# Two-layer recurrent attention with dense layers: the tokens' values loaded behind the transfer that turns P

## The chip, the cores and the metric

The kernel runs on one core of a Trainium2 chip. The metric is the time of one execution in device microseconds (us), as the median of several runs. A profile of one execution stands beside it: all rows of instructions, waits and DMA transfers below are from that one.

## The reference, cut to what matters

There are four layers: attention with a recurrent memory (A), a dense layer with a ReLU (B), A again and B again, each on the layer norm of its input and added to it. A works on segments of 32 tokens, one after another. The memory of 8 rows that a segment hands on is the first 8 rows of its output.

```python
for s in range(n_seg):                              # 64 segments of 32 tokens
    h = concat([mem, xs], axis=1)                   # 8 + 32 = 40 rows of 512
    q, k, v = (einsum('btd,dhe->bhte', h, W) for W in (Wq, Wk, Wv))   # 32 heads of 128
    p = softmax(where(mask, einsum(q, k) * scale, -1e9))
    o = einsum('bhte,hed->btd', einsum('bhqk,bhke->bhqe', p, v), Wo)
    mem, out_s = o[:, :8], o[:, 8:]
```

The segments of one layer form a chain through `mem`; B has no such chain.

## The kernel before, in words

The kernel goes through 68 steps. In step k the first attention layer (a = 0) works on segment k, and the second (a = 1) on segment k - 4, so that steps 4 to 63 hold both layers ("two-layer steps", 60 of them), and steps 0 to 3 and 64 to 67 hold one (`single`). Rows 0 to 39 of a tile belong to layer 0, rows 64 to 103 to layer 1. The order of the work on PE (TensorE), DVE (VectorE), SP (the queue that issues nearly all DMAs) and POOL (GpSimd) is the order in which the program is written; each engine takes its instructions in that order and waits at each for what it needs. ACT's (ScalarE's) order is left to the planner, by priority.

A two-layer step runs like this (lines in brackets):

- queries and keys of heads 0 to 15, from `HT` (`qk`, L575), into PSUM and out through ACT (L581) and DVE (L583);
- SP: the values of the tokens come into `Vs` from DRAM (`load_values`, L734). Values of tokens don't depend on the chain and are worked out steps ahead: for layer 0 in `values0` (L296, stored at L313 into `vd0`), or by riding along with the memory values (`vmds`), for layer 1 in `values1` at the end of the step before (L341, stored at L351 into `vd1`). `load_values` issues one DMA for layer 1 (L737), and for layer 0 one (L746) where k%4 is 2 or 3, or two (L742) where k%4 is 0 or 1. In all 512 KB come into `Vs`, in pieces of 1 KB;
- SP: the normalized rows are turned into `xnT` by a DMA transpose (`transpose_step`, L289), for the dense layer (`dense_h`, L507) and for tokens of later steps; then the values of the memory rows, just stored by `memory_values` (L770), come into the other rows of `Vs` (`load_memory_values`, L775, four DMAs of 32 KB);
- scores of heads 0 to 15 (L609) and their exponentials;
- queries and keys of heads 16 to 31. Behind their first batch, `probabilities` stands: it finishes the softmax of the first half (POOL writes `P_sb`, L646) and has SP turn it by a DMA transpose into `PT0` (`turn_p`, L663). Where k%4 is 3, `inputs_T` has SP turn the next inputs too (L248); `load_x` loads input rows from POOL's queue (L120);
- the dense layer, and the output matmuls of the step before (`output_x`, L365) or, where k%4 is 1, values of later tokens (`values0`, L306, and its stores, L313);
- scores and softmax of the second half, turned on PE (`transpose_p`, L656);
- `weighted_v` (L682): P times V. This reads `PT0`, `PT_sb` and `Vs`, whose rows are the weights that PE loads;
- the output matmul of the memory rows (L617), the new memory (`new_memory`, L820), the values of the next step's memory rows (L765), and the next step.

Of the kernel before, what the change touches and what calls it, by code (L numbers as in the profile page):

```python
# [22 lines left out]
def kernel(  # L23
# [48 lines left out]
    def has1(k):  # L72
        return DELTA <= k <= LAST
# [30 lines left out]
    def load_xb(n):  # L104
        tag, bufs = ("vst", 5) if n in (1, 2, 3) else ("xb", 1)
        xbs[n] = wk.tile([128, Dm], BF, tag=tag, bufs=bufs, name="xb")
        nc.sync.dma_start(out=xbs[n][:], in_=A_x[0, 128 * n:128 * n + 128, :])
# [117 lines left out]
    def normalize(eng, dst, src, mom, lo, hi):  # L225
        mv, rstd = mom
        eng.tensor_scalar(out=dst[lo:hi, :], in0=src[lo:hi, :], scalar1=mv[lo:hi, 0:1], scalar2=rstd[lo:hi, 0:1],
                          op0=ALU.subtract, op1=ALU.mult)

    def moments_x(n):  # L230
        stats = wk.tile([128, 6], F32, tag="ln_stats", bufs=1)
        nc.vector.bn_stats(out=stats[:], in_=xbs[n][:])
        return stat_tail(stats, "x")
# [47 lines left out]
    def layers(k):  # L281
        return [a for a in range(2) if (has0, has1)[a](k)]
# [306 lines left out]
    def qk(hf, act, between=None, behind=None):  # L589
        res = []  # L590
        for n, (o, nh) in enumerate(BATCHES):
            res.append((o, nh) + tuple(qk_batch(n, 16 * hf + o, nh, act[0], act[-1] + 1, None if n else between)))
            if n == 0 and behind:
                behind()
            if hf and n > 0:
                masks(*act[n - 1:n])
        return res
# [64 lines left out]
    def turn_p():  # L662
        nc.sync.dma_start_transpose(out=PT0[:], in_=P_sb[:].rearrange("p s k -> p (s k)"))  # L663
# [70 lines left out]
    def load_values(k, act):  # L734
        for a in act:
            if a == 1 or k == 1:
                nc.sync.dma_start(out=Vs[64 * a + M:64 * a + L, :].rearrange("t (n e) -> t n e", n=NCH),  # L737
                            in_=(vd1.pop(k) if a else vd0[0])[:].rearrange("i j t e -> t (i j) e"))
            elif k >= 4 and k % 4 < 2:
                for u in range(2):  # L740
                    lo = M + 2 * M * u
                    nc.sync.dma_start(out=Vs[lo:lo + 2 * M, :].rearrange("t (n e) -> t n e", n=NCH),  # L742
                                in_=vmds[k - k % 4 - 4 + 2 * (k % 4) + u][:, :, 2 * M:32, :].rearrange("i j t e -> t (i j) e"))
            else:
                r = SEG * (k % 2)
                nc.sync.dma_start(out=Vs[M:L, :].rearrange("t (n e) -> t n e", n=NCH),  # L746
                            in_=vd0[k // 2][:, :, r:r + SEG, :].rearrange("i j t e -> t (i j) e"))
# [8 lines left out]
    def memory_values(k, stage=(None, None), part=range(2)):  # L756
        if 0 in part:
            vmds[k] = dram.tile([2, 4, 32, 512], BF, tag="vmd", bufs=7, name="vmd")
        vmd = vmds[k]
        for ii in part:  # L760
            vp = ps_c.tile([128, 512], F32, tag="c", name="vm")
            for c4 in range(NC4):
                for j in range(4):
                    n = 4 * ii + j
                    nc.tensor.matmul(vp[32 * j:32 * j + 32, :], lhsT=HTm[:, c4, :],  # L765
                                     rhs=Wv_sb[:, c4, n * 512:(n + 1) * 512],
                                     start=(c4 == 0), stop=(c4 == NC4 - 1), tile_position=(0, 32 * j))
            VmS = wk.tile([128, 512], BF, tag="vst", bufs=5, name="VmS")[:] if stage[ii] is None else stage[ii]
            nc.scalar.copy(out=VmS, in_=vp[:])  # L769
            nc.sync.dma_start(out=vmd[ii].rearrange("j t e -> (j t) e"), in_=VmS)  # L770
# [124 lines left out]
    def step(k):  # L895
        act = layers(k)
        single = len(act) == 1
        cont = [a for a in act if k - DELTA * a + 1 < NSEG]
        n_x = k // 4 + 3
        has_x = n_x < NXT  # L900
        by_pe = k in (1, LAST)
        ahead = has1(k + 1) or not cont
        if k % 4 == 0 and has_x:
            load_xb(n_x)
        with tc.high_priority(offset=PRIO):
            behind = norm_rows.pop(k, None)
            if k == 1:
                def behind():
                    normalize(nc.vector, xbs[n_x], xbs[n_x], moments_x(n_x), 0, 128)
            qks = qk(0, act, behind=behind)  # L910
            load_values(k, act)
            if k == 1:
                memory_values(k)
                inputs_T(n_x, True)
        part = 4 if k == LAST else 8 if single else 5
        mid = 8 if k == LAST else 16

        light = split(k)
        block(k, 0, part)
        with tc.high_priority(offset=PRIO):  # L920
            transpose_step(k)
            load_memory_values(k, act)
            scores(qks, act)
            ess = exponentials(act)

        def probabilities():

            softmax(0, act, by_pe, ess)
            if not by_pe:
                turn_p()  # L930
            if k % 4 == 3 and has_x:
                inputs_T(n_x)
            if has0(k + 1):
                load_x(k + 1)
            if k == 1:
                load_dense()

        with tc.high_priority(offset=PRIO):
            qks = qk(1, act, behind=probabilities)
        if single:  # L940
            block(k, part, mid)
        elif light:
            dense_h(k - 2, slice(0, 1))
            block(k, part, 16)
        else:
            dense_h(k - 2)
        with tc.high_priority(offset=PRIO):
            scores(qks, act)
            softmax(1, act, by_pe)
        if single:  # L950
            dense_h(k - 2, slice(0, 1) if k == LAST else slice(None))
            block(k, mid, H)
            if k == LAST:
                keep_busy(3)
        elif light:
            dense_h(k - 2, slice(1, None))
            block(k, 16, H)
        else:
            block(k, part, H)
        f_mid = 9 if ahead or k == 2 else 5  # L960
        if k < LAST:
            dense_y(k - 2, 0, f_mid)
        if not single:
            add_output(k - 1)
        if k == LAST:
            add_last(k - 1, 0)
        if k % 4 == 1 and k > 1 and has_x:
            mom["x"] = moments_x(n_x)
        with tc.high_priority(offset=PRIO):
            transpose_p(1)  # L970
        if ahead and k < LAST:
            dense_y(k - 2, f_mid, NFC)
        tokens_in(k + 1)
        if k < LAST and spare_T(k + 1) is not None:
            nc.gpsimd.tensor_copy(out=HTm[:, :, 2 * M:32], in_=spare_T(k + 1))
        with tc.high_priority(offset=PRIO):
            pvs = weighted_v(act)
            outputs(k, pvs)
        if single and k < LAST and ahead:
            add_dense(k - 2)  # L980
            store(k - 2)
        if k == LAST:
            add_last(k - 1, 1)
            last_rows(k - 1, nc.gpsimd)
        elif single:
            add_output(k - 1, 0)
        if cont:
            with tc.high_priority(offset=PRIO):
                pool, tag = (ps_c, "c") if single else (ps_wo, "wo")
                wo = pool.tile([128, Dm], F32, tag=tag, name="wo")  # L990
                output_mem(k, wo)
        if not ahead:
            dense_y(k - 2, f_mid, NFC)
        if not single and k < LAST and ahead:
            add_dense(k - 2)
            store(k - 2)
        if cont:
            with tc.high_priority(offset=PRIO):
                new_memory(k, cont, wo)
        if single and k < LAST:  # L1000
            add_output(k - 1, 1)
        if not ahead:
            add_dense(k - 2)
            store(k - 2)
        values1(k + 1, 1)
        if cont:
            output_ride(k)
            with tc.high_priority(offset=PRIO):
                memory_values(k + 1)
        with tc.high_priority(offset=PRIO):  # L1010
            prepare(k + 1)
        if k % 4 == 2 and k > 2 and has_x:
            normalize(nc.vector, xbs[n_x], xbs[n_x], mom["x"], 0, 128)
# [88 lines left out]
```

## Time and profile before

| what | value |
|---|---|
| median of 3 runs | 1600.38 us (1595.73 to 1601.42) |
| the profiled execution | 1596.61 us; its span, first to last instruction, 1594.8 us |
| granted TensorE clock | 1.000 |
| busy: PE, PEld, DVE, ACT, POOL | 98%, 83%, 80%, 46%, 22% of the span |
| DMA queue q1 (SP's transfers) | 136.09 MB, 37.6% of 16 engines' span |
| DMA queue q8 (instructions) | 335 packets of 16 KB, 5.49 MB |
| from one step's first read of `Vs` on PE to the next's | 23.0 to 23.6 us in most two-layer steps |

How to read it: PE is TensorE's matmuls, PEld its weight loads, which overlap them. SPq is SP's own sequence of instructions, where the issue of a DMA stands with the time that the issue took; when the bytes move and land is not in that row. A DMA's landing is the last update of its semaphore in the trace. The share of DMA in a row of windows is the mean busy share of 16 DMA engines. "A <- B" names what an engine waited for.

### The profile page before, as it was taken

To read this page: it belongs to the slowest core of one execution; us is meant where nothing else is said; L and a number is where in the kernel's file an instruction comes from. 1 tells how busy PE (TensorE), PEld (TensorE's weight loads), DVE (VectorE), ACT (ScalarE), POOL (GpSimd) and SP (SyncE) were. 2 spreads that over 40 slices of the span, in tenths; PEclk is the share of its full clock that TensorE was granted. 3 is DMA by queue.
4 is the path that set the end of the run, shared out by engine and by line. 5 is a ranking of instruction groups with operands and counts; after the bars stand their busy time and mean duration, and the time that the engine had idled before them with its cause. 6 is when DMAs were issued, how large, how long until landed. Compare 5 with 4: busy or idle time off the path is not lost.

```text
span 1594.8 us, 94682 instructions
## 1 busy us (share of the span) xinstructions
PE 1565.9 (98%) x42680; PEld 1320.7 (83%) x42680; DVE 1268.4 (80%) x3115; ACT 738.9 (46%) x1799; POOL 349.8 (22%) x670
## 2 busy tenths in 40 slices
PE   6999999999999999999999999999999999999998
PEld 4677888888898888889888888988888898898886
DVE  4578888888888888888888888888878888887866
ACT  3434444444544544454454545445454544545433
POOL 2012222222222222222222222222222222222110
PEclk9999999999999999999999999999999999999999
DMA  9733343343343534444334443343443333233332
GB/s 369 237 78 74 76 87 89 65 98 86 77 78 83 94 64 95 84 73 87 83 87 71 98 83 77 84 83 82 80 98 79 74 88 79 78 77 93 70 75 41
DMA packets 222564, 146.38 MB, mean 92 GB/s; under 512 B 124008, under 2 KB 216528, under 8 KB 222160
## 3 DMA queue, kind: packets, MB, share of 16 engines
q1 hardware_dynamic: 218992, 136.09, 37.6%
q8 instruction: 335, 5.49, 1.5%
q0 software_dynamic: 3072, 4.20, 1.1%
q14 instruction: 69, 0.57, 0.1%
q10 hardware_dynamic: 96, 0.03, 0.0%
HBM read 65.41 MB, written 45.35 MB: 69 GB/s over the span
## 4 chain that ended last, share of the span: by engine, by line
PE 96%; DMA 2%; DVE 1%; SPq 1%; issue 0%; ACT 0%; POOL 0%; POOLq 0%; ACTq 0%
PE qp L575 38%; PE wox L365 10%; PE wo L617 8%; PE vm L765 7%; PE v L346 7%; PE hp L507 6%; PE sp L528 5%; PE pv L682 4%; PE sp L609 4%; PE vp L306 3%; DMA Wv_sb<-in_A_Wv_dram 2%; PE tp L656 1%; PE xp L478 1%; PE wox L388 1%; SPq L134 0%; PE mt L820 0%
## 5 line engine op out<-in xcount | busy, mean ns | idle before, releaser
L581 ACT CAST QT<-qp 128x480 bf16<-128x480 f32 (+3 forms) x408 | 201.7, 494 | 392.3 <-PE qp L575 392.2
L575 PE MATMUL qp<-HT,Wq_sb 128*128 128x80 bf16 (+1 forms) x8704 | 370.2, 200 | 2.1 <-POOL HT L754 1.2
L575 PE MATMUL qp<-HT,Wk_sb 128*128 128x80 bf16 (+1 forms) x8704 | 369.2, 199 | 1.5 <-DMA Wk_sb<-in_A_Wk_dram 0.7
L575 PEld LDWEIGHTS <-Wq_sb 128*128 128x128 bf16 x8704 | 325.6, 100 | 33.8 <-issue 26.5
L575 PEld LDWEIGHTS <-Wk_sb 128*128 128x128 bf16 x8704 | 328.2, 100 | 2.3 <-DMA Wk_sb<-in_A_Wk_dram 1.2
L583 DVE CAST KT<-qp 128x480 bf16<-128x480 f32 (+3 forms) x408 | 231.4, 568 | 124.0 <-PE qp L575 118.1
L646 POOL TENSOR_TENSOR P_sb<-es,sm 128x320 bf16<-128x320 f32 x185 | 130.9, 721 | 751.7 <-ACT es L631 502.2
L365 PE MATMUL wox<-Wo_sb,OTx 128*64 128x256 bf16 x2880 | 173.6, 273 | 0.0
L625 DVE TENSOR_REDUCE mx<-sp 128x8 f32<-128x320 f32 x256 | 115.0, 487 | 73.6 <-PE sp L609 72.7
L365 PEld LDWEIGHTS <-OTx 128*64 128x64 bf16 x2880 | 150.2, 110 | 2.9
L631 ACT ACTIVATE es<-es 128x320 f32<-128x320 f32 x256 | 110.7, 469 | 58.2 <-DVE es L629 57.2
L765 PE MATMUL vm<-Wv_sb,HTm 128*32 128x512 bf16 x2176 | 136.4, 380 | 0.6 <-DVE HT L834 0.6
L641 DVE TENSOR_REDUCE sm<-es 128x8 f32<-128x320 f32 x256 | 118.3, 462 | 15.0 <-ACT es L631 4.7
L617 PE MATMUL wo<-Wo_sb,OTm 128*32 128x512 bf16 x2144 | 128.9, 380 | 0.2 <-issue 0.2
L346 PE MATMUL v<-Wv_sb,xnT 128*32 128x512 bf16 x2048 | 129.0, 378 | 0.0
L601 DVE CAST sp<-maskb 128x320 f32<-128x320 bf16 x256 | 118.4, 484 | 0.0
L629 DVE TENSOR_TENSOR es<-sp,mx 128x320 f32<-128x320 f32 x256 | 113.8, 483 | 1.5
L765 PEld LDWEIGHTS <-HTm 128*32 128x32 bf16 x2176 | 90.6, 96 | 27.4 <-issue 12.3
L528 PE MATMUL sp<-w_sb,hT 128*64 128x256 bf16 (+4 forms) x1452 | 104.1, 275 | 0.2 <-issue 0.2
L769 ACT CAST VmS<-vm 128x512 bf16<-128x512 f32 x134 | 78.6, 587 | 53.8 <-PE vm L765 53.8
L507 PE MATMUL hp<-xnT,w_sb 128*128 128x64 bf16 (+3 forms) x2948 | 102.2, 193 | 0.5 <-DVE xnT L436 0.4
L507 PEld LDWEIGHTS <-w_sb 128*128 128x128 bf16 (+1 forms) x2948 | 95.1, 101 | 1.3 <-issue 0.7
(124 smaller groups left out, 2028.8 us busy)
## 6 DMA issues: line engine op xcount, KB each, us to landing
Vs<-vd SPq DMA_DIRECT2D x96, 256.0 KB
vd<-vst SPq DMA_DIRECT2D x181, 128.0 KB
vmd<-VmS SPq DMA_DIRECT2D x134, 128.0 KB
Vs<-vmd SPq DMA_DIRECT2D x254, 32.0 KB
Vs<-vmd SPq DMA_DIRECT2D x60, 128.0 KB
Wq_sb<-in_A_Wq_dram SPq DMA_DIRECT2D x2, 2048.0 KB
Wk_sb<-in_A_Wk_dram SPq DMA_DIRECT2D x2, 2048.0 KB
Wv_sb<-in_A_Wv_dram SPq DMA_DIRECT2D x2, 2048.0 KB
```

The lines of the kernel that those rows point to most:

```text
L346: nc.tensor.matmul(vp[32 * j:32 * j + 32, :], lhsT=tokens[:, c4, :], rhs=Wv_sb[:, c4, n * 512:(n + 1) * 512], start=(c4 == 0), stop=(c4 == ...
L365: nc.tensor.matmul(out[64 * j:64 * j + nr, 0:256], lhsT=lhsT, rhs=rhs[:, 256 * j:256 * j + 256], start=start, stop=stop, tile_position=(0, ...
L507: nc.tensor.matmul(hp[0:fs, fc - f0, 0:n], lhsT=w1_sb[:, c4, fc * 128:fc * 128 + fs], rhs=cols(c4), start=(c4 == 0), stop=(c4 == NC4 - 1))
L528: nc.tensor.matmul(sp_banks[bank][64 * j:64 * j + n, 0:w], lhsT=hT_tiles[d][0:fs, fc, 0:n], rhs=w2_flat[0:fs, fc * Dm + 256 * j:fc * Dm + ...
L575: nc.tensor.matmul(qp[:, hi, 0:ncol], lhsT=W_sb[:, c4, h * Dh:(h + 1) * Dh], rhs=HT[:, c4, a_lo:a_hi, :], start=(c4 == 0), stop=(c4 == NC4 ...
L581: nc.scalar.copy(out=dst[:, 0:nh, a_lo * L:a_hi * L], in_=qp[:, 0:nh, 0:ncol])
L583: nc.vector.tensor_copy(out=dst[:, 0:nh, a_lo * L:a_hi * L], in_=qp[:, 0:nh, 0:ncol])
L601: nc.vector.tensor_copy(out=sp_tiles[a], in_=maskb2)
L617: nc.tensor.matmul(wo[32 * j:32 * j + 32, :], lhsT=OTm[:, h, n, 2 * M * c:2 * M * c + 4 * M], rhs=Wo_sb[:, h, :], start=(h < 4), stop=(h > ...
L641: nc.vector.tensor_reduce(out=sm[:], in_=es[:], axis=AX.X, op=ALU.add)
L646: eng.tensor_tensor(out=P, in0=es[:], in1=sm[:].unsqueeze(2).to_broadcast([128, 8, L]), op=ALU.mult)
L765: nc.tensor.matmul(vp[32 * j:32 * j + 32, :], lhsT=HTm[:, c4, :], rhs=Wv_sb[:, c4, n * 512:(n + 1) * 512], start=(c4 == 0), stop=(c4 == NC ...
```

## The change

In steps with one layer nothing changes. In two-layer steps `load_values` is called later: no longer right behind the first half's queries and keys, but inside `probabilities`, behind `turn_p`. On SP the two or three loads so move past the transpose into `xnT` (L289), the four loads of the memory's values (L775) and the transpose into `PT0` (L663), and stand ahead of the inputs' transpose (L248) and of the stores of later tokens' values (L313). What is loaded, from where and into which rows stays as it was.

```diff
             qks = qk(0, act, behind=behind)
-            load_values(k, act)
+            if single:
+                load_values(k, act)
             if k == 1:
                 memory_values(k)
                 inputs_T(n_x, True)
...
             softmax(0, act, by_pe, ess)
             if not by_pe:
                 turn_p()
+            if not single:
+
+                load_values(k, act)
             if k % 4 == 3 and has_x:
                 inputs_T(n_x)
             if has0(k + 1):
```

## The prediction

> **What bounds the kernel now.** I read the page's busy times and its chain of waits first. The columns of the first row are the engine, its busy time, its share of the span and its instructions.
>
> ```profile
> PE 1565.9 (98%) x42680; PEld 1320.7 (83%) x42680; DVE 1268.4 (80%) x3115; ACT 738.9 (46%) x1799; POOL 349.8 (22%) x670
> ...
> PE 96%; DMA 2%; DVE 1%; SPq 1%; issue 0%; ACT 0%; POOL 0%; POOLq 0%; ACTq 0%
> ```
>
> TensorE is the bound. DMA's 2% of the chain is the first 38 us, when the weights come in. Whether TensorE waits for anything inside the two-layer steps (k = 4 to 63, 110 to 1511 us) is told by the waits of PE in that window: who waited for whom, us in total, times, longest.
>
> ```profile
> PE tp L656 <- POOL HT L754: 0.9, 1, 0.9
> PE tp L656 <- DVE P_sb L646: 0.8, 1, 0.8
> PE qp L575 <- issue: 0.3, 1, 0.3
> PE wo L617 <- issue: 0.2, 1, 0.2
> ```
>
> That is 2.2 us in 1400, and no wait for a DMA. So **no transfer of these steps is late today, and making one earlier can give back 2 us at most.** The change can only be paid for by a transfer that becomes late.
>
> Next the SP queue over one such step, k = 30 (start, length of the issue, line, transfer):
>
> ```profile
> 717.76 0.88 SPq L770 DMA_DIRECT2D vmd<-VmS  x2
> 718.74 0.40 SPq L746 DMA_DIRECT2D Vs<-vd  x1
> 719.31 0.37 SPq L737 DMA_DIRECT2D Vs<-vd  x1
> 719.78 1.20 SPq L289 DMA_TRANSPOSE xnT<-XN  x1
> 721.07 1.46 SPq L775 DMA_DIRECT2D Vs<-vmd  x4
> 727.24 1.24 SPq L663 DMA_TRANSPOSE PT<-P_sb  x1
> ```
>
> and, from the timeline of weight loads in the same step, the place where the loaded values are read:
>
> ```profile
> 732.90 0.15 PEld L528 LDWEIGHTS <-hT 128*64 128x64 bf16 x4
> 733.25 0.44 PEld L682 LDWEIGHTS <-Vs 40*128 40x128 bf16 x29 [0.20 <-issue]
> ```
>
> The two loads (L746, L737) are issued 14.5 us before `Vs` is read. Call T the issue of the transfer that turns P (L663). The first read stands at T+6.01 here; over the 60 steps the median is T+6.24, and T+5.87 where k%4 is 1.
>
> **The change, part by part.** *Taken from the beginning:* two issues (0.40 and 0.37 us, 1.0 us with their gaps) or, where k%4 is 0 or 1, three (some 1.4 us). They stood ahead of `xnT` (L289) and the memory values (L775) on SP, which move forward by as much. Their readers, `hp` and the same L682, wait for neither now; worth 0, at most the 2 us above.
>
> *Put behind L663:* the same issues. L663 takes 1.24 us and the next issue follows 0.09 us later (in step 31 L248 follows at T+1.33). The issues start 0.43 to 0.57 us apart where there are two; with three, the last starts some 1.05 us after the first. So **the last load is issued at T+1.83 (two) or T+2.38 (three)**, and cannot be earlier, since SP stands at L663 until POOL has written P. Behind them SP has only L248 (k%4 = 3, read two steps later) and the `vst` stores (k%4 = 1, each buffer reused five allocations on), then nothing until the next store, 11 us after T. That costs nothing.
>
> *The added wait* is TensorE's, at L682. Everything later in the step is queued behind it on PE, and PE has no slack to make it up: each microsecond of lateness is paid whole.
>
> *How long a load takes* is in the trace's semaphore updates: a DMA's landing is the last of the updates of its semaphore. From the issue of the last load of a step to the last landing, before:
>
> | k%4 | loads | min, median, max us | last issue after | read (median) | late steps of 15 | late us in sum |
> |---|---|---|---|---|---|---|
> | 0 | 3 | 3.20, 3.91, 5.37 | T+2.38 | T+6.24 | 8 | 5.0 |
> | 1 | 3 | 3.16, 3.77, 5.01 | T+2.38 | T+5.87 | 10 | 6.9 |
> | 2 | 2 | 3.08, 4.08, 4.90 | T+1.83 | T+6.24 | 4 | 2.0 |
> | 3 | 2 | 3.36, 4.00, 5.36 | T+1.83 | T+6.24 | 6 | 3.3 |
>
> The last two columns give each step its own old latency at the new place, and take what it exceeds that step's own read. Sum: **17 us**, over 28 of 60 steps.
>
> Is the old latency right in the new place? Ahead of the loads stood two 128 KB writes (L770); now it is the turning of P, 256 KB. Windows of step 30 show it (the last two columns are the DMA share and GB/s):
>
> ```profile
> 727.25:728.50 1.25, 1.25 (x54) 1.20 (x53) 0.72 (x2) 0.51 (x3) 0.49 (x1) 1.00 0.01 3
> 728.50:729.75 1.25, 1.25 (x48) 1.25 (x42) 1.07 (x3) 0.47 (x1) 0.00 (x0) 1.00 1.21 267
> 729.75:733.25 3.50, 3.50 (x76) 3.23 (x72) 3.21 (x9) 1.12 (x3) 1.62 (x4) 1.00 0.01 2
> ```
>
> The turning moves its bytes from T+1.3 to T+2.5; the first packets of a load come some 1.4 us after its issue (step 31: issue 741.79, packets from 743.0 on and in number from 743.5), so at T+2.7. It has passed by then, and 3.5 us of empty queues follow: room for 512 KB, which at the 260 GB/s of the first loads take 2.0 us. The old latency can stand. One thing is worse. Instruction packets (queue q8, 16 KB, each 0.9 to 1.5 us on one DMA engine) fall at T+2.2 to T+4.2 in nearly every step. Where one covered over 0.5 us of the stretch 0.8 to 3.0 us after the last load's issue, the latency was 4.5 us on average (18 steps), else 3.9. At the new place 43 steps are so covered: 25 more, by 0.6 us each, 15 us, of which some 4 lie beyond the read. **17 + 4 = 21 us.**
>
> Ends for this price: with every load at the shortest latency of its class none is late, 0 us; with every one at the longest, 15 x (1.51 + 1.52 + 0.49 + 0.95) = 67 us. I take 21, as it rests on the same transfers step by step.
>
> The Trainium skill ("DMA: Bandwidth & Descriptors", section "Queues, rings and completion order") says that each DMA engine takes one queue's descriptors in ring order, so the loads start behind the turning even when it is held up. The trace agrees in kind: in step 33 the turning lands at T+4.79 and the `vst` store issued at T+1.59 lands behind it, at T+4.95, against T+3.37 in step 9, where the turning lands at T+3.07.
>
> **The rivals.**
>
> *The loads are in time.* Nothing waits if the last landing comes within 4.4 us of the last issue (two loads; 6.24 less 1.83), or 3.9 and 3.5 us (three). For it: medians of 4.0 to 4.1 and 3.9, 3.8 lie at that point, and no `xnT` and no memory values follow on the heels of the loads. Against it: the instruction packets, and k%4 = 1. If latencies shrink by 0.5 us, some 6 us stay; then also up to 2 us of old waits could go: 1600 to 1607 us, the case that is not slower. The Trainium skill has a rule on this side (same page, "Anatomy of one DMA — SWDGE (gpsimd) path"): a transfer costs about 2.0 us and its bytes at 436 GB/s, fitted for another issuing path than SP's; by that, as an estimate, 512 KB are there 3.2 us after the last issue and nothing is late. The trace has 3.1 us as its shortest case, not its usual one.
>
> *The turning drags.* In 16 of 60 steps it lands at T+4.5 or later, 1.5 us behind the others, an instruction packet being in its way. If that delay and the loads' own simply add, or the loads begin only when the turning has landed (median T+3.46, and 512 KB with their landing 3.1 to 3.5 us on), the last landing is at T+6.6 to T+7: 0.4 to 0.8 late with a median turning and 1.5 more in the 16: 60 x 0.6 + 16 x 1.5 = 60 us, 1660.
>
> *Faster by over 0.5%* would need 8 us of waits to go, where the rows show 2.
>
> **How the numbers follow.** The profiled execution took 1596.6 us (span 1594.8 and 1.8 around it); with 21 it is 1617.6. The median of the runs shown stands 3.8 above it, at 1600.4, and gives 1621; I say 1620. Chances: forecast (8 to 40 us lost) 0.63; in time 0.25; drags 0.09; faster 0.03. The range from 1599 to 1645 leaves out most of the last two and a little of the first. Within 0.5% (8 us, about what a measurement of this kernel can tell from no change) lies the second case alone: slower 0.72, same 0.25, faster 0.03.
>
> **What would show it.** In the changed kernel's profile the waits of PE and PEld should have a new row at L682 released by the load of `Vs`, 0.2 to 0.8 us each in half the steps or more, most with k%4 = 1; the distance from first read to first read should grow by that and by nothing else. `xnT` should land a microsecond earlier, with no effect. I am wrong if L682 shows no wait (then the latency fell), if nearly all steps wait a microsecond (then the turning drags), or if the time goes at another line.

## The result, and the profile after

The changed kernel takes 1657.2 us (median of 6 runs, 1649.1 to 1660.8) against 1599.4 us before (1595.7 to 1601.7): 1.0356 times, with a 95% interval of 1.0332 to 1.0381. I had said 1620, at most 1645. The sign was right, the size was not. The profiled execution took 1649.1 us, with a span of 1647.4, 52.6 more than before; it is the quickest of the six, so between the medians the loss is 57.8 us, some 5 more than the profile shows.

The page of the changed kernel, rows of busy time and of the chain (shares of the span by engine, then by line):

```profile
PE 1580.8 (96%) x42680; PEld 1325.4 (80%) x42680; DVE 1270.3 (77%) x3115; ACT 737.3 (45%) x1799; POOL 349.0 (21%) x670
...
PE 64%; DMA 16%; SPq 7%; issue 5%; POOL 4%; ACT 3%; DVE 1%; ACTq 0%; POOLq 0%
PE qp L575 26%; DMA Vs<-vd 13%; PE wo L617 8%; PE vm L765 7%; PE v L346 7%; SPq L663 4%; PE wox L365 4%; POOL P_sb L646 4%; PE pv L682 3%; ACT es L631 2%; PE sp L609 2%; SPq L742 2%; PE hp L507 2%; DMA Wv_sb<-in_A_Wv_dram 2%; PE sp L528 1%
```

TensorE held 96% of the chain before. Now the chain runs through the load of `Vs` (13%) and back from it to its issue (SPq, L663 and L742) and to P itself (POOL, L646). The waits of PE in the two-layer steps had no DMA in them; now they read

```profile
PE pv L682 <- DMA Vs<-vd: 28.7, 41, 1.7
PE pv L682 <- DMA Vs<-vmd: 4.0, 5, 1.1
PE pv L682 <- issue: 2.4, 6, 0.8
PE pv L682 <- DMA vd<-vst: 1.7, 4, 0.8
```

All four are at L682. `Vs<-vmd` are layer 0's loads where there are two of them; the four waits that the view puts down to the store `vd<-vst` end 0.02 to 0.16 us after the last load's landing. A usual step is read from its SP queue and its weight loads, here k = 50, where T is 1241.55:

```profile
1241.55 1.24 SPq L663 DMA_TRANSPOSE PT<-P_sb  x1
1242.84 0.57 SPq L746 DMA_DIRECT2D Vs<-vd  x1
1243.47 0.45 SPq L737 DMA_DIRECT2D Vs<-vd  x1
```

```profile
1247.79 0.09 PEld L682 LDWEIGHTS <-Vs 40*128 40x128 bf16 x1 [0.20 <-issue]
1248.52 0.87 PEld L682 LDWEIGHTS <-Vs 40*128 40x128 bf16 x63 [0.63 <-DMA Vs<-vd]
```

The first weight load comes at T+6.24 as before: layer 0's rows are there. The second reads layer 1's, and stands 0.63 us for the load issued at T+1.92. By the semaphore's updates that one lands at T+6.93: 15 of the 16 DMA engines by 1247.44, the last at 1248.48. The windows of the same stretch (last two columns DMA share and GB/s):

```profile
1242.81:1244.06 1.25, 1.25 (x51) 1.25 (x50) 0.84 (x3) 0.60 (x1) 0.00 (x0) 1.00 1.16 253
1244.06:1245.31 1.25, 1.25 (x28) 1.25 (x26) 1.11 (x4) 0.77 (x2) 0.00 (x0) 1.00 0.87 228
1245.31:1246.56 1.25, 1.25 (x28) 1.23 (x24) 1.15 (x5) 0.10 (x1) 0.61 (x1) 1.00 0.82 192
```

The first row is the turning of P; the loads follow on its heels and take the two other rows and a thin tail.

**Where the 52.6 us are.** For every step I took the time from the last matmul ahead of L682 to the first of L617, before and after. This stretch grew by more than 0.1 us in 54 of 60 steps, by 46.3 us in all. The rest of the steps grew by 7.0 us, and five stretches of 3.4 us in which TensorE was granted half its clock account for that (below).

### The profile page after: what moved, and what is told of

Its sections match the earlier page's. It is cut to its first block, busy times and chain, and to the rows that moved or that the text cites. A ratio compares the mean times of both kernels' runs of the same rounds, so it can differ in the third digit from the quotient of the medians.

```text
span 1647.4 us, 94615 instructions
## 1 busy us (share of the span) xinstructions
PE 1580.8 (96%) x42680; PEld 1325.4 (80%) x42680; DVE 1270.3 (77%) x3115; ACT 737.3 (45%) x1799; POOL 349.0 (21%) x670
## 4 chain that ended last, share of the span: by engine, by line
PE 64%; DMA 16%; SPq 7%; issue 5%; POOL 4%; ACT 3%; DVE 1%; ACTq 0%; POOLq 0%
PE qp L575 26%; DMA Vs<-vd 13%; PE wo L617 8%; PE vm L765 7%; PE v L346 7%; SPq L663 4%; PE wox L365 4%; POOL P_sb L646 4%; PE pv L682 3%; ACT es L631 2%; PE sp L609 2%; SPq L742 2%; PE hp L507 2%; DMA Wv_sb<-in_A_Wv_dram 2%; PE sp L528 1%
## 5 line engine op out<-in xcount | busy, mean ns | idle before, releaser
L646 POOL TENSOR_TENSOR P_sb<-es,sm 128x320 bf16<-128x320 f32 x185 | 130.7, 720 | 751.8 <-ACT es L631 519.2
L617 PE MATMUL wo<-Wo_sb,OTm 128*32 128x512 bf16 x2144 | 133.8, 392 | 0.4
L682 PEld LDWEIGHTS <-Vs 40*128 40x128 bf16 x4096 | 64.9, 93 | 56.7 <-DMA Vs<-vd 26.8
L700 DVE CAST OTm<-pv 128x96 bf16<-128x96 f32 (+4 forms) x273 | 65.8, 278 | 48.9 <-PE pv L682 45.6
```

Source lines behind the costliest of these rows:

```text
L617: nc.tensor.matmul(wo[32 * j:32 * j + 32, :], lhsT=OTm[:, h, n, 2 * M * c:2 * M * c + 4 * M], rhs=Wo_sb[:, h, :], start=(h < 4), stop=(h > ...
L646: eng.tensor_tensor(out=P, in0=es[:], in1=sm[:].unsqueeze(2).to_broadcast([128, 8, L]), op=ALU.mult)
```

## The experiments

T is the issue of the transfer that turns P, as in the prediction. Ratios are against the kernel before.

**e1: ahead of the turning.** The same loads, still in the middle of the step, one place earlier on SP:

```diff
         def probabilities():
 
+            if not single:
+                load_values(k, act)
             softmax(0, act, by_pe, ess)
             if not by_pe:
                 turn_p()
-            if not single:
-
-                load_values(k, act)
```

> In the two-layer steps the loads stay behind xnT and the memory values, in the middle of the step, but one place earlier on SP than in the changed kernel: ahead of the transfer that turns P. Theory A (the loads are late because SP stands at L663 until P is written, so that they are issued at T+1.3 or later): they go out right behind L775, some 4 us before T, land before T+2, and the time is that of before, 0.995 to 1.005 of it. Rival (the price is for moving 512 KB into the second half of the step, beside the turning): then the turning lands late behind the loads, L682 still waits, and 10 us or more of the loss of 58 us stay.

Measured: 0.9988 (0.9979 to 0.9998), 1595.6 us. SP's timeline in step 50:

```profile
1185.54 1.49 SPq L775 DMA_DIRECT2D Vs<-vmd  x4
1187.07 0.31 SPq L746 DMA_DIRECT2D Vs<-vd  x1
1187.73 0.92 SPq L737 DMA_DIRECT2D Vs<-vd  x1
1192.72 1.24 SPq L663 DMA_TRANSPOSE PT<-P_sb  x1
```

The loads go out 5 us before T and land at T-0.5 on average, T+1.6 at the latest. The whole loss is gone. Theory A holds: neither the middle of the step nor the place behind `xnT` and the memory values costs anything; being queued behind an instruction that waits for P does.

**e8: e1 once more.**

> The kernel of e1 once more, with five rounds, since it came out 0.9988 of before: either it is a little faster (0.997 to 0.9995, some 2 us: the 2.2 us of waits of TensorE in the two-layer steps or the shorter way to xnT), or the same and the first interval was chance.

Measured: 0.9995 (0.9986 to 1.0004), 1595.9 us. It can't be told from the kernel before.

**e2 and e3: half of the loads.** In e2 layer 0's loads are late, in e3 layer 1's:

```diff
-            if single:
-                load_values(k, act)
+            load_values(k, act if single else [1])      # e3: [0]
...
             if not single:
-
-                load_values(k, act)
+                load_values(k, [0])                     # e3: [1]
```

> Only layer 0's loads (one of 256 KB or two of 128 KB) go behind the turning of P; layer 1's load stays at the beginning of the step. Theory V (the last landing is set by 512 KB coming through behind the turning): half the bytes land at T+4.0 to T+5.6, as the first loads of the changed kernel do (issue to landing 3.9 to 4.1 us from T+1.3 and T+1.9), so in nearly all steps in time: 1600 to 1608 us. Rival H (what counts is that a load stands behind the turning and the instruction packet, whatever its size): a third or more of the loss stays, 1618 us or more.

> The mirror: only layer 1's load (one of 256 KB in every step) goes behind the turning. By theory V it is issued at T+1.3 and lands at T+4.9 to T+5.7: in time, 1600 to 1606 us, a little better than with layer 0 late, where k%4 = 0 and 1 issue two loads. By rival H as there, 1618 us or more.

Measured: e2 1.0073 (1.0054 to 1.0092), 1609.7 us, a little over what theory V gave; e3 1.0017 (1.0008 to 1.0027), 1600.3 us. The last landing falls from T+6.93 in the mean to T+5.73 and T+5.43, and the stretch of L682 grows by 7.7 and 2.2 us. In e3 two waits for the load are left among the waits of PE:

```profile
PE pv L682 <- DMA Vs<-vd: 1.4, 2, 0.8
```

8 and 2 us for the halves, 46 for both: it is not a price per load but a threshold. Half of the loads behind the turning are nearly always in time, all of them are not. Rival H is out. Two things move the landing forward: the last issue is earlier (T+1.84 and T+1.41 in the mean, against T+2.37), and from there to the landing it takes 3.89 and 4.02 us, no more than at the old place, though the whole turning is still ahead.

**e4: the same loads from POOL's queue.**

```diff
-    def load_values(k, act):
+    def load_values(k, act, queue=nc.sync):
...
-                nc.sync.dma_start(
+                queue.dma_start(
...
             if not single:
-
-                load_values(k, act)
+                load_values(k, act, nc.gpsimd)
```

> The same loads at the same place of the program as in the changed kernel, but issued from POOL's queue, behind POOL's writing of P: not behind the turning on SP nor in its DMA queue. Theory B (the turning ahead in the same queue and its 1.24 us of issue make the loads late): the loads start some 1.2 us earlier and beside the turning, and most of the loss goes: under 1625 us. Rival (16 DMA engines move 256 KB of turning and 512 KB of loads in the same 5 us whatever the queue; theory V): both land late, 1640 us or more. POOL's own issue takes time in which HT and HTm copies could wait; a wait at L754 would show that.

Measured: 1.0445 (1.0409 to 1.0481), 1668.8 us. The waits of PE, and the issues on POOL (KB each, median us to landing):

```profile
PE pv L682 <- DMA PT<-P_sb: 31.5, 35, 2.4
PE pv L682 <- DMA Vs<-vd: 11.8, 24, 1.2
```

```profile
Vs<-vd POOLq DMA_DIRECT2D x90, 256.0 KB, 5.7
```

The loads are no longer behind the turning, so now the turning is late, and a load takes 5.7 us beside it. Getting out of the queue doesn't help here, and theory B's 1625 us are missed. How much of the 5.7 us is POOL's own way of issuing is not shown: no run has these loads on POOL without the turning beside them. With e2 and e3, e4 speaks for theory V, that 256 KB of P and 512 KB of values don't come through in the time there is, whatever the queue; that the bytes alone decide is argued, and e9 narrows it.

**e9: one eighth of the turning.** This kernel turns only the first 32 KB of P; the rest of `PT0` stays old.

```diff
-        nc.sync.dma_start_transpose(out=PT0[:], in_=P_sb[:].rearrange("p s k -> p (s k)"))
+        nc.sync.dma_start_transpose(out=PT0[:, 0:1, :], in_=P_sb[:, 0, :])
```

> The changed kernel, but the transfer that waits for P turns only the first of P's eight blocks (32 KB and not 256): seven eighths of the turning are left out, and what is read in their place is old. SP still waits for P at L663. Theory V (256 KB of turning and 512 KB of loads together take longer than the 6.2 us between P and its use): with the turning nearly gone the loads are issued some 1 us earlier and take 4.1 us or less from the last issue to the last landing, not 4.56 as in the changed kernel, and the time is under 1610 us. Rival (the new place itself, with its instruction packets and the POOL load beside it, makes a load slow): the latency stays at 4.5 us or more, and only the earlier issue helps, 1605 to 1625 us.

Measured: 1.0178 (1.0151 to 1.0206), 1624.8 us. Theory V's 1610 is missed: the time lies at the upper end of the rival's range, the latency between the two. One thing in both was wrong: the issue of the turning is hardly shorter. This is its row by line (ns, min/median/max; 1232/1242/2735 in the changed kernel):

```profile
L663 SPq DMA_TRANSPOSE PT<-P_sb x65: 1115/1127/2619, 78.5 to 1587.3; - x65
```

So the loads are issued 0.11 us earlier, not 1 us, and what the experiment takes out is mainly the turning's bytes. Latency from the last issue falls from 4.56 to 4.27 us in the mean (4.10 before the change), the last landing from T+6.93 to T+6.53, and the growth at L682 from 46.3 to 26.7 us. The waits show it:

```profile
PE pv L682 <- DMA Vs<-vd: 15.9, 24, 1.5
```

Of the 0.40 us by which the loads land earlier, 0.29 are latency and 0.11 the issue. So some 20 us of the loss go with seven eighths of the turning, most of them for its bytes ahead of the loads; the other 27 stay when little more than the place of the issue, behind L663, is left.

**e5 and e6: moving the instruction packets.** 48 or 96 idle matmuls while TensorE waits for the first weights:

```diff
         tp = transpose_pe(mem0)
+        shift = ps_fill.tile([128, Dm], F32, tag="fill", name="shift")
+        for _ in range(48):                             # e6: 96
+            nc.tensor.matmul(shift[:, 0:64], lhsT=ident[:], rhs=ident[:, 0:64], start=True, stop=True)
```

> The changed kernel with 48 idle matmuls (96 instructions of TensorE) in front of the first step, where TensorE waits for weights anyway: nothing changes in the steps but the place of the 16 KB instruction packets, which come every 256 instructions of TensorE and so move some 1.5 us forward in each step, from the loads (T+2.2 to T+4.5) into the turning. Theory C (a packet on one DMA engine makes that engine's share of the loads late): lateness and time move by 10 us or more against the changed kernel. Theory V (512 KB behind the turning are too much for 4.4 us, wherever the packet falls): the time stays within 8 us of the changed kernel's 1657.

> The same with 96 idle matmuls (192 instructions): the packets fall some 1 us later than in the changed kernel, on the end of the loads. Theory C: later landings, 10 us or more above the changed kernel. Theory V: within 8 us of it.

Measured: e5 1.0419 (1.0401 to 1.0436), 1665.1 us; e6 1.0325 (1.0309 to 1.0341), 1647.9 us. e5 is 8 us slower and e6 9 us quicker than the changed kernel (10 and 5 by the ratios), the other way round from theory C, and at or just past the 8 us of theory V. Two things show why. The packets did not move as I had reckoned: of those that start between T and T+6, 41 of 61 start at T+2 to T+4 in the changed kernel, 35 of 63 in e5, 22 of 67 in e6. And L682's stretch grew by nearly the same, 49.4 and 43.3 us against 46.3. Most of the difference is the clock: 11 stretches at half clock in e5 and 17.9 us lost outside L682, 3 and 3.7 us in e6, 5 and 7.0 us in the changed kernel.

The traces also show a place where the packets matter that no theory had: the issue. In 15 of the changed kernel's 60 steps a packet starts between T-0.2 and T+1.15, while SP issues the turning. In all 15 the last load is issued over 0.1 us later than usual, by 0.81 us on average; in the other 45 steps, once. In e6 a packet falls there in 29 steps, and in 26 of them the issue is late: the mean last issue goes from T+2.37 to T+2.53, the latency from 4.56 to 4.34 us, and the landing hardly moves (T+6.93, T+6.87). Why the issue is late beside a packet, and what share of the latency the packets have, stays open.

**e7: idle matmuls in place of the wait.**

```diff
         with tc.high_priority(offset=PRIO):
+            if not single:
+                keep_busy(4)
             pvs = weighted_v(act)
```

> The changed kernel with four idle 128x512 matmuls (0.86 us by L893 and L765 rows of 0.22 us each) ahead of weighted_v in two-layer steps, where TensorE stands still for 0.8 us on average. If halved-clock stretches of the changed kernel come from that standstill, they vanish here (five of 3.4 us before, some 8 us of loss). The time: 60 x 0.86 = 52 us for the idle matmuls, and what exceeds 0.86 us of waits, some 10 us, on 1597: 1650 to 1665 us, the same as the changed kernel within 10 us, since idle work only takes the place of waiting. If the waits were not spare time, it would be 1657 + 52.

Measured: 1.0382 (1.0368 to 1.0397), 1658.8 us. No stretch of halved clock is left in the profile, all four runs were granted the full clock, and 52 us of idle work (the estimate of the expectation) have cost 2 us against the changed kernel, 4 by the ratios. Among the waits of PE this is left of those for a load:

```profile
PE pv L682 <- DMA Vs<-vd: 3.5, 7, 0.8
```

TensorE's time at L682 was spare, and filling its standstill ends the halving of the clock.

## Why the prediction was wrong, step by step

*What bounds the kernel, and what an earlier transfer can give: right.* e1 issues `xnT` and the memory values early as the changed kernel does and ends within 0.2% of before.

*The place of the wait: right.* All of the waiting is at L682, it is paid whole, and L682 is the only line of PE with new waits. e1 undoes it by the order on SP alone.

*The last issue: right in the median, short in the mean.* I had T+1.83 and T+2.38. The medians are T+1.93 and T+2.39. I missed that in 12 of 60 steps the first load goes out only at T+1.4 to T+2.8, and that in 4 more a later one is held up, so that the mean over all steps is T+2.37 and not T+2.10: 0.26 us. The kernel before had it in its row for L663 (ns, min/median/max), of which I took the middle number:

```profile
L663 SPq DMA_TRANSPOSE PT<-P_sb x65: 1232/1244/2616, 79.3 to 1557.4; - x65
```

In 15 of its 60 steps the issue took over 1.3 us, and the mean was 1.45.

*The latency: this step failed.* "It has passed by then" and "The old latency can stand" were the words; I gave the loads their old 4.10 us. They took 4.56. I had reasoned from rates: the turning's bytes end at T+2.5, a load's first packets come 1.4 us after its issue, so the two miss each other. In step 50 they do (turning's windows, then the loads'), and still the landings are later. What I had put too low is the time for the bytes themselves, 2.0 us at 260 GB/s. In the 45 steps with k%4 not 1, where no stores of later values follow, the 512 packets of 1 KB start 1.36 us after the first issue, as I had reckoned, but run from T+2.79 to T+6.33 in the mean, 3.5 us. In e9, with an eighth of the turning, the latency is shorter by 0.3 of the 0.46 us; with half of the loads (e2, e3) all of the 0.46 is gone. So most of it takes the turning and all 512 KB together. By which way the one slows the other, whether in the DMA engines or on the road to DRAM, no run here shows. Together with the later issue the last landing is T+6.93 where my table meant T+6.20.

*Why 0.7 us made 46 out of 17.* My own table said that the median step had 0.3 to 0.4 us to spare or was up to 0.3 late. At such a place a shift makes nearly every step late. The table itself gives the result: with every landing 0.73 us later its 17 us and 28 late steps become 46.5 us and 53 steps; measured are 46.3 and 54. The later issue alone would make 25 us, the longer latency alone 33. I did name both ends, 0 and 67 us, and then put the range's end at 45, below the bound that the rows gave. e2 and e3 are the same threshold from its other side.

*The clock: not in the sum at all.* It is 7.0 us in the profile, and 17.9 in e5. The 5 us between the profile and the median go with it too, by the granted clock of the runs: 0.995 in the profiled one, 0.990 in those of 1658.3 and 1660.8 us, 0.992 and 0.993 in the three between. As an estimate from these, 0.990 is some ten stretches of 3.4 us instead of five, and at 1.4 us each 7 us more.

*The instruction packets: my 4 us rest on nothing that the runs confirm.* Before the change the steps so covered took 4.5 us against 3.9; in the changed kernel, by the same split, 40 steps took 4.56 and the other 20 took 4.57. Where a packet does go with a late load is ahead of it, at the issue (e5 and e6).

*The rivals.* "The loads are in time" is out. "The turning drags" gave 1660 us, which is 3 us off, and that is luck, for the trace does not bear out its reason: the turning lands at T+4.5 or later in 24 steps, but where the loads' issue was not held up, the last landing is T+6.46 in such two-load steps and T+6.69 in the others, and T+7.02 and T+6.86 with three loads. The loads do not wait for the turning's landing, only take longer behind its bytes. The rule of the Trainium skill that I weighed beside the first rival ("DMA: Bandwidth & Descriptors", section "Anatomy of one DMA — SWDGE (gpsimd) path"; 2.0 us and the bytes at 436 GB/s) is for loads issued from POOL's queue: e4 has such loads, with 5.7 us in the median beside the turning where the rule, as an estimate, gives 2.6. The measurement decides.

## What to carry to other kernels

A DMA that could go at once should not stand, on its queue, behind one that waits for a late result: its issue is then as late as that result, whatever its own data. Where a transfer's old margin becomes a few tenths of a microsecond in the median step, try the table with every landing some tenths later before settling the range, and take the range as far as the rows' own bound. Take the mean of an issue's length, not its median, where the tail is paid. And look at the time between the trigger and the use as room for all the bytes that come through in it: in e4 another queue did not make it wider.

## What the runs showed of the hardware

**A standstill of 1.5 us can cost 1.4 us more.** The windows of the changed kernel around 614 us (length, PE busy first; the last three columns are granted clock, DMA share, GB/s):

```profile
610.40:613.90 3.50, 1.50 (x43) 1.08 (x39) 1.70 (x4) 0.42 (x1) 0.92 (x4) 1.00 0.47 86
613.90:617.30 3.40, 3.40 (x87) 1.94 (x89) 2.75 (x10) 1.60 (x7) 0.00 (x0) 0.50 0.02 5
617.30:620.70 3.40, 3.40 (x80) 1.93 (x76) 1.54 (x4) 1.87 (x4) 1.21 (x2) 1.00 0.13 41
```

TensorE idles for 2.0 of 3.5 us, and for the next 3.4 us its clock is halved; the output matmul's mean there is 610 ns (its row of 613.9 to 617.3 below) where the whole run has 392:

```profile
L617 PE MATMUL wo<-Wo_sb,OTm 128*32 128x512 bf16 x24 | 2.6, 610 | 0.0
```

The five stretches last 3.4 us each and start 27.3, 51.2, 27.3 and 99.0 us apart, all multiples of 3.413. The windows ahead of them had 1.3 to 2.0 us of idle time, but so had one without effect:

```profile
487.60:491.00 3.40, 1.65 (x44) 1.29 (x40) 1.83 (x4) 0.42 (x1) 1.14 (x4) 1.00 0.85 123
```

so the idle time of a window alone does not always decide. It nearly does: on the same grid of 3.413 us every other window of the two-layer steps that was not followed by half the clock had at most 1.24 us of idle time. In e5 eleven windows with 1.29 to 1.88 us were followed by it and none with 1.21 or less; in e4 and e6 some of 1.3 to 1.6 us had no effect. The Trainium skill ("TensorE: Matmul & The Clock Gate", section "HAM oscillation — how this bites in real kernels") warns of gaps over 3.4 us; here no gap ahead of a halved clock was longer than 1.6 us in the changed kernel.

**The issue of a DMA transpose costs SP nearly the same for 32 KB as for 256 KB:** 1.13 against 1.24 us in the median.
